# A two-dimensional Fourier mix and a low-rank mixer on one core: the second batch's low-rank step one loop step later, its lines drained by two engines, and the last chunk's output buffers in another pool

## The chip, the cores and the metric

The kernel runs on one core of a Trainium2 chip. The metric is the device time of one execution in microseconds. Five executions of the kernel before are known; beside them there is one execution taken with a profile, which has a time of its own.

## The reference

The input x has 8 batches of 3136 rows and 256 columns. What is computed, cut to what matters:

```python
X = fft(fft(x, axis=1), axis=2).real          # batch, 3136, 256
h = (X^T @ U @ V)^T                           # rank 32, along the 3136 rows
u = X + h
out = u + relu(u @ w_ch1) @ w_ch2             # w_ch1: 256 x 1024, w_ch2: 1024 x 256
```

## The kernel before, in words

The 3136 rows are taken as 49 x 64, so the transform along them is done in two stages: stage one over the 49, on lines of 64, and stage three over the 64, one line for each of 25 values k1 (0 to 24; the mirrored lines come out of the same products as "minus" lines). Batches are worked in four pairs.

**The tiles.** For a batch, `g` holds what stage three reads: partitions 0 to 63 are the stage-one results, partitions 64 to 127 hold the low-rank contribution (64 to 95 for the first 129 columns, 96 to 127 for the rest), the same for each k1. So that stage three can add the low-rank part by the same matmul, 64 rows of `te` (the input's projection on U) are spread over all 25 k1 of `g`. `q` holds the finished lines u of a pair, as the columns of the MLP.

**The main loop.** Each pair has 13 chunks of up to 512 rows, and each chunk takes 4 steps `t`, so a pair has 52 steps, numbered 0 to 51. In a step the program issues, in this order: `mlp1` of the present chunk (L375: 8 matmuls into `hps`, drained by ScalarE with a relu into `hT`, L385), `mlp2` of the chunk before (L387: 8 matmuls of 256 columns and two of 128 into `ops`), then the extra steps that a plan has put there, and last the drain of `ops` (ScalarE copies half into `om`, L406; VectorE writes sum and difference into `ob`, L407 and L408; four stores to HBM from SP, L412). The drain comes at every second step. In the last chunk it comes at every step, with two stores, some of them from ScalarE's queue. The order on every engine is the order of the program: the schedule is manual.

**The plan** (`plan`, L780) is a table of 52 lists. `place(steps, lo, hi)` spreads steps evenly over the slots from lo to hi. In the first pair, which differs from the others, the extras around the change are:

- `turned_steps` (L239), steps 10 to 17: stage one of the second batch by another route (L227 `tps`, 32 narrow matmuls), ScalarE copies into `zt`, and at every second step eight VectorE copies write rows of `g` (L76, `quarter_rows`). The last eight come at step 17.
- `te_single` (L293), step 18: 50 narrow matmuls (L298) of `us` with rows 0 to 63 of `g`, then two VectorE copies into `te` (L269, L270) and three GpSimd copies that spread it over k1 0 to 8, 9 to 16 and 17 to 24 of `g` (L306). This is the low-rank step of the second batch.
- `s3_steps` (L314), 13 steps over 19 to 30: stage three of the second batch (L322). A step takes one group of four k1 and one block of columns, into a PSUM tile of the pool `psd`, and drains it into `q`: as one copy of 128x512 for groups 1 to 5, as two copies of up to 128x256 for group 0, and two of 128x128 in the last step. The two steps of group 0 share a slot. The copies are made by the function handed in.
- `place_next` (L789): loads of the next pair's x (SP loads `xa`, GpSimd gathers `xb`, L99), folds on GpSimd (L144, L145) and on VectorE (L134 to L136) and stage one of the next pair (L185), drained by ScalarE (L73), at steps 17, 18, 19, 20, 22, 23 and on.
- `load_uz`, step 24: two loads from SP (L777).

Matmul outputs of `te_single`, `s3_steps`, stage one and `turned_steps` all take turns in the two buffers of `psd`.

`copy_dve` copies on VectorE. `copy_alt` takes ScalarE and VectorE in turn, beginning with ScalarE; one counter serves all its uses, and the first batch's lines, which use it in steps 1 to 8, leave it even.

**Output buffers.** `ob` comes from `opool`, tag "ob", with four buffers; `xa` comes from `xpool`, tag "xa", with four buffers.

Of the kernel before, what the change touches and what calls it, by code (L numbers as in the profile page):

```python
# [10 lines left out]
FP32 = mybir.dt.float32  # L11
# [11 lines left out]
def kernel(  # L23
# [10 lines left out]
    B, S, D = x.shape  # L34
    R = moe_U.shape[1]
    H = moe_w_ch1.shape[1]
    P = 128
# [10 lines left out]
    xpool = ctx.enter_context(tc.tile_pool(name="xpool", bufs=4))  # L48
# [218 lines left out]
    def te_out(pr, b, ps, c0, s0, spread):  # L267
        te = tes[b]
        nc.vector.tensor_copy(te[64:96, 0:129], ps[c0:c0 + 32, 0, 0:129])  # L269
        nc.vector.tensor_copy(te[96:128, 129:256], ps[s0:s0 + 32, 0, 129:256])  # L270
        spread(pr.g[b], te)
# [21 lines left out]
    def te_single(pr, b, spread, ps=None):  # L293

        ps = ps or psd.tile([P, 2, D], FP32, tag="ps", name="teps")
        for k in range(NK1):
            for s, cs in enumerate([slice(0, 129), slice(129, 256)]):
                nc.tensor.matmul(ps[32 * s:32 * s + 32, 0, cs], us[:, k, s::2], pr.g[b][0:64, k, cs],  # L298
                                 start=(k == 0), stop=(k == NK1 - 1))
        te_out(pr, b, ps, 0, 32, spread)  # L300

    def spread(parts):
        def run(g, te):
            src = te[64:128].bitcast(I32)
            for eng, k0, k1 in parts:
                eng.tensor_copy(g[64:128, k0:k1].bitcast(I32), src.unsqueeze(1).to_broadcast([64, k1 - k0, D // 2]))  # L306
        return run

    def two(row, a, b, n):

        v = row[:, a:a + n]
        return bass.AP(row.tensor, v.offset, [list(v.ap[0]), [b - a, 2], [1, n]])

    def s3_steps(pr, b, evac):  # L314

        if pr.q is None:
            pr.q = qpool[pr.p % 2].tile([P, 2, 6272], BF16, tag="q", name="q")

        def mm(o, k1, blk, st, rows=P, low=None):
            lt = low[:, blk::2] if low is not None else pr.g[b][0:rows, k1, blk::2]  # L320
            r = T[0:rows, k1, 0:64] if k1 == 0 else T[0:rows, k1, :].rearrange("p (s j) -> p s j", s=2)
            nc.tensor.matmul(o, lt, r, start=st, stop=True, skip_group_check=True)  # L322

        def lines(ps, g, blk, rows, low=None):
            for u in range(4):
                us = slice(u * 64, (u + 1) * 64)
                mm(ps[:, 0, us] if 4 * g + u == 0 else ps[:, :, us], 4 * g + u, blk, u == 0 and low is None, rows, low)

        def step(g, blk):
            ps = psd.tile([P, 2, 256], FP32, tag="ps", name="ps")  # L330
            lines(ps, g, blk, P)
            move(ps, g, blk, evac)

        def move_part(ps, g, blk, evac, part):
            lo = 64 if part and g == 0 else 0
            c0 = 3200 + b * 1536 + (4 * g - 1) * 64 if part else b * 1600 + 4 * g * 64
            evac(pr.q[:, blk, c0 + lo:c0 + 256], ps[:, part, lo:256])

        def move(ps, g, blk, evac):
            if g == 0:  # L340
                move_part(ps, g, blk, evac, 0)
                move_part(ps, g, blk, evac, 1)
            else:
                k0 = 4 * g
                evac(two(pr.q[:, blk, :], b * 1600 + k0 * 64, 3200 + b * 1536 + (k0 - 1) * 64, 256), ps[:])

        def last():
            ps = psd.tile([P, 2, 2, 64], FP32, tag="ps", name="ps")
            k1 = NK1 - 1
            for blk in range(2):  # L350
                mm(ps[:, blk], k1, blk, blk == 0)
            for blk in range(2):
                evac(two(pr.q[:, blk, :], b * 1600 + k1 * 64, 3200 + b * 1536 + (k1 - 1) * 64, 64), ps[:, blk])

        yield lines, move_part
        for g in range(6):
            for blk in range(2):
                yield lambda g=g, blk=blk: step(g, blk)
        yield last
# [27 lines left out]
    def mlp2(ch, t, last=False):  # L387
        q, nt = ch.pr.q, len(ch.units) // 2
        if t % 2 == 0 or last:
            ch.po = pso.tile([P, 2, 2, P], FP32, tag="o", name="ops")  # L390
        ps = ch.po[:, 0 if last else t % 2]
        tk = slice(ch.c0 + t * P, ch.c0 + (t + 1) * P)
        for j in range(JT):
            nc.tensor.matmul(ps, ch.h[:, j, t * P:(t + 1) * P], W2[:, j, :],  # L394
                             start=(j == 0 and (t % 2 == 0 or last)), stop=(j == JT - 1), skip_group_check=True)
            if j < 2:
                nc.tensor.matmul(ps[:, j], q[:, j, tk], (Bp if ch.sg > 0 else Bm)[:, j], start=False, stop=False,  # L397
                                 skip_group_check=True)
        if not (last or t % 2 == 1 or t == nt - 1):
            return lambda: None  # L400

        def drain():
            n = 1 if last else t % 2 + 1
            ob = opool.tile([P, 2, D], FP32, tag="ob", name="ob")
            om = opool.tile([P, 2, P], FP32, tag="om", bufs=2, name="om")
            nc.scalar.copy(om[:, 0:n], ch.po[:, 0:n, 1])  # L406
            nc.vector.tensor_tensor(ob[:, 0:n, 0:P], ch.po[:, 0:n, 0], om[:, 0:n], op=AL.add)  # L407
            nc.vector.tensor_tensor(ob[:, 0:n, P:D], ch.po[:, 0:n, 0], om[:, 0:n], op=AL.subtract)  # L408

            def store(i, hf, engine):  # L410
                b, r0 = ch.units[2 * (t - n + 1 + i) + hf]
                engine.dma_start(out=out[b].rearrange("(k2 k1) d -> k1 k2 d", k1=N1)[r0],  # L412
                                 in_=ob[hf * 64:(hf + 1) * 64, i])

            if not last or t == 0:
                for i in range(n):
                    for hf in range(2):
                        store(i, hf, nc.sync)
            else:
                store(0, 0, nc.sync)  # L420
                late.append(lambda: store(0, 1, nc.scalar))
            while last and late and (t == 1 or t == nt - 1):
                late.pop(0)()
        return drain
# [307 lines left out]
    opool = ctx.enter_context(tc.tile_pool(name="opool", bufs=4))  # L732
# [8 lines left out]
    spread_pool = spread([(nc.gpsimd, 0, 9), (nc.gpsimd, 9, 17), (nc.gpsimd, 17, NK1)])  # L741
# [38 lines left out]
    def plan(p):  # L780

        at = [[] for _ in range(NS)]

        def place(steps, lo, hi):
            steps = list(steps)
            for i, s in enumerate(steps):
                at[lo + i * (hi - lo) // len(steps)].append(s)

        def place_next(nx, a, gap, s3lo):  # L789

            s1 = list(s1_steps(nx, copy_act))
            for c, (load, fn, fd) in enumerate(load_steps(nx)):
                for o, f in [(0, load), (4, fn), (7, fd), (9, s1[2 * c]), (10, s1[2 * c + 1])]:
                    at[int(a + gap * c) + o].append(f)
            e = int(a + gap * 7) + 11
            place([lambda: (turn(nx, 0, [(0, 8), (8, NK1)]), turn(nx, 1, whole))], e, e + 1)
            place(te_steps(nx, spread_pool), e, e + 2)
            place(list(s3_steps(nx, 0, copy_dve))[1:], s3lo, NS)

        cur = pairs[p]  # L800
        if p == 0:
            rest = []
            for t, f in zip([1, 2, 2, 3, 4, 5, 5, 6, 8], s3b0[4:]):
                at[t].append(f)
            at[0].append(lambda: w2_fold(0))
            at[2].append(lambda: w2_fold(1))
            place([late_tables], 8, 9)
            place([load_uz], 24, 25)
            place([lambda: rest.append(pair_tables())], 6, 7)
            place([lambda: rest[0]()], 10, 11)  # L810
            place(turned_steps(cur, 1, X1), 10, 18)
            place([lambda: te_single(cur, 1, spread_pool)], 18, 19)
            place(list(s3_steps(cur, 1, copy_dve))[1:], 19, 31)
            place_next(pairs[1], 8, 2.6, 44)
        else:
            place(list(s3_steps(cur, 1, copy_dve))[1:], 3, 18)
            if p + 1 < NP:
                place_next(pairs[p + 1], 0, 3.4, 40)
        return at

    for i in range(len(chunks) + 1):
        cur = chunks[i] if i < len(chunks) else None
# [47 lines left out]
```

## Time and profile before

| | |
|---|---|
| median of five runs | 454.09 us (451.43 to 456.57) |
| the profiled execution's own time | 453.86 us |
| its span, first to last instruction | 452.1 us |
| mean granted TensorE clock | 0.993 |
| TensorE matmul busy | 427.7 us, 95% of the span |
| ScalarE busy | 290.5 us, 64% |
| VectorE busy | 224.3 us, 50% |
| GpSimd busy | 143.1 us, 32% |

How to read it: PE is TensorE's matmuls, PEld its weight loads, DVE is VectorE, ACT is ScalarE, POOL is GpSimd, SP is the engine that issues most of the DMAs. L298 means line 298 of the kernel. In a row of the timeline come the start and the length in microseconds, the engine, the line, the operation, what is written <- what is read, the shapes, how many; in brackets, how long the engine had been idle before it, and what it waited for. The granted clock is the share of TensorE's full speed that it was given.

### The profile page before, as it was taken

To read this page: it belongs to the slowest core of one execution; us is meant where nothing else is said; L and a number is where in the kernel's file an instruction comes from. 1 tells how busy PE (TensorE), PEld (TensorE's weight loads), DVE (VectorE), ACT (ScalarE), POOL (GpSimd) and SP (SyncE) were. 2 spreads that over 40 slices of the span, in tenths; PEclk is the share of its full clock that TensorE was granted. 3 is DMA by queue.
4 is the path that set the end of the run, shared out by engine and by line. 5 is a ranking of instruction groups with operands and counts; after the bars stand their busy time and mean duration, and the time that the engine had idled before them with its cause. 6 is when DMAs were issued, how large, how long until landed. Compare 5 with 4: busy or idle time off the path is not lost.

```text
span 452.1 us, 10536 instructions
## 1 busy us (share of the span) xinstructions
PE 427.7 (95%) x4158; PEld 309.5 (68%) x4221; DVE 224.3 (50%) x541; ACT 290.5 (64%) x402; POOL 143.1 (32%) x180
## 2 busy tenths in 40 slices
PE   3889997999999998999999999999999999999995
PEld 1656665777767776776867777767767777666763
DVE  7773686765345467563354356563354345222222
ACT  5886653777565576777466666777466665666662
POOL 7465355841330546360420444560410000000000
PEclk9999998999999999999999999999999999999998
DMA  8749753875592646763682548763662222222323
GB/s 150 159 134 170 205 157 104 246 195 173 148 241 65 171 117 221 224 186 117 162 213 66 146 128 247 220 190 118 159 141 71 71 63 62 76 71 72 86 56 93
DMA packets 59761, 64.34 MB, mean 142 GB/s; under 512 B 12950, under 2 KB 52672, under 8 KB 59552
## 3 DMA queue, kind: packets, MB, share of 16 engines
q1 hardware_dynamic: 50000, 42.68, 36.7%
q0 software_dynamic: 7232, 14.30, 13.3%
q10 hardware_dynamic: 2480, 6.69, 3.9%
q8 instruction: 33, 0.54, 0.5%
q14 instruction: 16, 0.13, 0.1%
HBM read 34.62 MB, written 32.19 MB: 148 GB/s over the span
## 4 chain that ended last, share of the span: by engine, by line
PE 85%; DVE 6%; DMA 4%; issue 2%; SPq 1%; POOL 1%; ACT 1%; DVEq 0%; POOLq 0%
PE ops L394 35%; PE hps L383 34%; PE ps L322 5%; PE ops L397 4%; PE ps L185 2%; DMA out_dram<-ob 2%; PE teps L284 1%; SPq L412 1%; DMA w_f<-in_moe_w_ch_dram 1%; PE tps L227 1%; DVE g L76 1%; PE teps L298 1%; ACT hT L385 1%; DVE q L76 1%; DVE ob L408 1%
## 5 line engine op out<-in xcount | busy, mean ns | idle before, releaser
L385 ACT ACTIVATE hT<-hps 128x1024 bf16<-128x1024 f32 (+1 forms) x208 | 202.5, 975 | 110.4 <-PE hps L383 103.6
L394 PE MATMUL ops<-W,hT 128*128 128x256 bf16 x1568 | 225.3, 273 | 1.1 <-DVE ob L408 0.9
L394 PEld LDWEIGHTS <-hT 128*128 128x128 bf16 x1568 | 145.4, 98 | 35.4 <-DVE ob L408 0.8
L76 DVE CAST q<-ps 128x512 bf16<-128x512 f32 (+3 forms) x121 | 65.1, 559 | 87.3 <-PE ps L322 81.6
L383 PE MATMUL hps<-q,W1p 128*128 128x512 bf16 (+1 forms) x420 | 103.2, 355 | 2.3 <-DVE q L76 0.5
L407 DVE TENSOR_TENSOR ob<-ops,om 128x256 f32<-128x256 f32 (+1 forms) x102 | 41.8, 410 | 114.7 <-ACT om L406 112.3
L383 PE MATMUL hps<-q,W1m 128*128 128x512 bf16 x351 | 96.4, 381 | 2.2 <-ACT hT L385 0.5
L144 POOL TENSOR_TENSOR y<-xa,xb 98x510 f32<-98x510 f32 (+1 forms) x48 | 61.1, 1294 | 109.1 <-DMA xa<-in_x_dram 87.3
L383 PEld LDWEIGHTS <-W1p 128*128 128x128 bf16 x448 | 40.3, 97 | 26.9 <-issue 1.7
L383 PEld LDWEIGHTS <-W1m 128*128 128x128 bf16 x384 | 35.5, 98 | 27.0 <-issue 2.0
L397 PEld LDWEIGHTS <-q 128*128 128x128 bf16 x392 | 38.5, 98 | 21.7 <-issue 1.2
L406 ACT COPY om<-ops 128x256 f32<-128x256 f32 (+1 forms) x102 | 37.3, 365 | 13.7 <-PE ops L394 7.9
L306 POOL COPY g<-te 64x1024 int32<-64x1024 int32 (+1 forms) x23 | 24.8, 1119 | 57.4 <-DVE te L270 52.8
L408 DVE TENSOR_TENSOR ob<-ops,om 128x256 f32<-128x256 f32 (+1 forms) x102 | 41.1, 403 | 0.0
L73 ACT CAST z<-ps 128x512 bf16<-128x512 f32 x48 | 28.1, 586 | 18.8 <-PE ps L185 17.6
L397 PE MATMUL ops<-Bp,q 128*128 128x128 f16 x200 | 38.4, 219 | 0.0
L322 PE MATMUL ps<-T,g 128*128 128x128 bf16 (+3 forms) x400 | 36.9, 218 | 0.3 <-ACT q L73 0.3
L397 PE MATMUL ops<-Bm,q 128*128 128x128 f16 x192 | 37.1, 220 | 0.0
L322 PEld LDWEIGHTS <-g 128*128 128x128 bf16 (+1 forms) x400 | 29.5, 98 | 4.5 <-DVE q L76 0.4
L99 POOL DMA_INDIRECT xb<-in_x_dram,idx x24 | 24.4, 1018 | 5.4 <-issue 4.3
L185 PE MATMUL ps<-yb,F 98*128 98x258 bf16 (+1 forms) x108 | 19.2, 268 | 1.7 <-DVE q L76 1.7
L76 DVE COPY g<-zt 32x400 bf16<-32x400 bf16 (+3 forms) x45 | 17.0, 378 | 7.2 <-ACT zt L73 6.5
(136 smaller groups left out, 210.8 us busy)
## 6 DMA issues: line engine op xcount, KB each, us to landing
out_dram<-ob SPq DMA_DIRECT2D x389, 64.0 KB
xa<-in_x_dram SPq DMA_DIRECT2D x24, 392.0 KB
zturn<-z ACTq DMA_DIRECT2D x9, 512.0 KB
g<-zturn SPq DMA_DIRECT2D x3, 800.0 KB
g<-zturn SPq DMA_DIRECT2D x3, 544.0 KB
X<-in_x_dram POOLq DMA_DIRECT2D x4, 384.0 KB, 8.2
X<-in_x_dram POOLq DMA_DIRECT2D x2, 744.0 KB
zturn<-z ACTq DMA_DIRECT2D x3, 448.0 KB
```

What stands on the lines that cost most here:

```text
L73: nc.scalar.copy(o, i)
L76: nc.vector.tensor_copy(o, i)
L144: nc.gpsimd.tensor_tensor(ck.y[:, l0:l1, 1:256], ck.xa[:, l0:l1, 1:256], rb[:, l0:l1, 255:0:-1], op=AL.add)
L185: nc.tensor.matmul(o[..., cs], F[:, 2 * t + i].rearrange("p b k c -> p (b k c)"), y[..., cs], start=first, stop=True, skip_group_check=True)
L322: nc.tensor.matmul(o, lt, r, start=st, stop=True, skip_group_check=True)
L383: nc.tensor.matmul(ps[:, i, 0:n], (W1p if ch.sg > 0 else W1m)[jp // 2][:, blk, j], q[:, blk, c0:c0 + n], start=(blk == 0), stop=(blk == 1))
L385: nc.scalar.activation(ch.h[:, 2 * jp:2 * jp + 2, 0:n], ps[:, :, 0:n], AF.Relu)
L394: nc.tensor.matmul(ps, ch.h[:, j, t * P:(t + 1) * P], W2[:, j, :], start=(j == 0 and (t % 2 == 0 or last)), stop=(j == JT - 1), skip_group ...
L397: nc.tensor.matmul(ps[:, j], q[:, j, tk], (Bp if ch.sg > 0 else Bm)[:, j], start=False, stop=False, skip_group_check=True)
L406: nc.scalar.copy(om[:, 0:n], ch.po[:, 0:n, 1])
L407: nc.vector.tensor_tensor(ob[:, 0:n, 0:P], ch.po[:, 0:n, 0], om[:, 0:n], op=AL.add)
L408: nc.vector.tensor_tensor(ob[:, 0:n, P:D], ch.po[:, 0:n, 0], om[:, 0:n], op=AL.subtract)
```

## The change

Two places are changed in the first pair's plan: the low-rank step of the second batch is put at step 19 instead of 18, and its stage three is spread over steps 20 to 30 instead of 19 to 30, drained by ScalarE and VectorE in turn instead of by VectorE alone. And in the last chunk of the kernel the output buffers are taken from the pool and tag of the x loads instead of the output pool.

```diff
         def drain():
             n = 1 if last else t % 2 + 1
-            ob = opool.tile([P, 2, D], FP32, tag="ob", name="ob")
+            ob = (xpool.tile([P, 2, D], FP32, tag="xa", name="ob") if last else
+                  opool.tile([P, 2, D], FP32, tag="ob", name="ob"))
             om = opool.tile([P, 2, P], FP32, tag="om", bufs=2, name="om")
...
             place(turned_steps(cur, 1, X1), 10, 18)
-            place([lambda: te_single(cur, 1, spread_pool)], 18, 19)
-            place(list(s3_steps(cur, 1, copy_dve))[1:], 19, 31)
+            place([lambda: te_single(cur, 1, spread_pool)], 19, 20)
+            place(list(s3_steps(cur, 1, copy_alt))[1:], 20, 31)
             place_next(pairs[1], 8, 2.6, 44)
```

With 13 stage-three steps over 11 slots, slots 20 and 25 get two of them and the others one.

## The prediction

> **What bounds the kernel now.** I read the page first: TensorE is busy 427.7 of 452.1 us and the chain that ended last is 85% PE, so only time in which PE idles or runs slowly can be won. Then the waits by engine, for the places where PE idles behind another engine, then the timeline and the half-microsecond windows of the one place that stands out. From the list of waits (us in total, times, longest):
>
> ```profile
> PE ps L185 <- DVE q L76: 1.7, 2, 1.1
> PE teps L298 <- DVE g L76: 1.5, 1, 1.5
> DVE ob L407 <- DMA out_dram<-ob: 1.3, 3, 0.5
> ```
>
> The second row is the step that the change moves; one of the two waits of the first row lies right behind it; the third is what the output buffers touch. The timeline there (start, length, engine, then what; idle before it in brackets):
>
> ```profile
> 69.16 3.04 DVE L76 COPY g<-zt 32x400 bf16<-32x400 bf16 x8 [0.89 <-ACT zt L73]
> ...
> 69.95 0.82 PE L394 MATMUL ops<-W,hT 128*128 128x256 bf16 x6
> 72.25 1.61 PE L298 MATMUL teps<-g,us 64*32 64x129 bf16 x50 [1.49 <-DVE g L76]
> ...
> 74.63 1.49 PE L383 MATMUL hps<-q,W1m 128*128 128x512 bf16 x3 [0.22 <-issue]
> 75.00 3.12 POOL L306 COPY g<-te 64x1152 int32<-64x1152 int32 x3 [4.60 <-issue]
> ...
> 77.48 0.56 PE L322 MATMUL ps<-T,g 128*128 128x64 bf16 x8
> 77.88 1.28 DVE L76 CAST q<-ps 128x256 bf16<-128x256 f32 x4 [3.00 <-PE ps L322]
> 78.62 0.40 PE L185 MATMUL ps<-yb,F 98*128 98x258 bf16 x2 [0.59 <-DVE q L76]
> ```
>
> Step 18 of the first pair: PE is through with both MLP halves at about 70.7 and stands until 72.25, because the low-rank step needs rows of g that DVE is still copying (eight copies, 69.16 to 72.20). What comes after is slow too. The windows (busy us of PE, PEld, DVE, ACT, POOL; then granted clock):
>
> ```profile
> 73.30:73.80 0.50, 0.50 (x20) 0.37 (x15) 0.50 (x3) 0.00 (x0) 0.00 (x0) 0.89 0.00 0
> 73.80:74.30 0.50, 0.50 (x4) 0.37 (x4) 0.47 (x3) 0.00 (x0) 0.00 (x0) 0.50 0.00 0
> ...
> 76.30:76.80 0.50, 0.50 (x6) 0.38 (x4) 0.00 (x0) 0.50 (x1) 0.50 (x1) 0.50 0.28 74
> 76.80:77.30 0.50, 0.50 (x5) 0.41 (x4) 0.00 (x0) 0.38 (x1) 0.50 (x2) 0.70 0.36 90
> ```
>
> The clock is 0.50 from about 73.75 to 77.1, some 3.4 us, and nowhere else in the main loop (the page's row of clocks has its one low digit there). From the end of the kernel:
>
> ```profile
> 447.89 0.29 DVE L407 TENSOR_TENSOR ob<-ops,om 128x128 f32<-128x128 f32 x1 [0.47 <-DMA out_dram<-ob]
> 448.10 0.28 DVE L408 TENSOR_TENSOR ob<-ops,om 128x128 f32<-128x128 f32 x1
> ...
> 448.34 0.54 SPq L412 DMA_DIRECT2D out_dram<-ob  x1
> 448.97 0.55 SPq L412 DMA_DIRECT2D out_dram<-ob  x1
> ```
>
> The last drain waits for an earlier store, yet SP, which issues the stores, follows on one after another from 443.93 and reaches the last only at 448.97.
>
> **What the Trainium skill says.** (1) "TensorE: Matmul & The Clock Gate", Part 1: the array runs at half rate after a quiet window of about 3.4 us, until a busy one has passed, and the windows run free of the kernel. The trace agrees: 0.50 for 3.4 us after a gap of 1.5 us followed by 1.6 us of narrow matmuls. (2) The same page, "Architectural detail": ScalarE and VectorE are strict FIFO. It agrees: the low-rank step's te copy at 74.28 starts behind the ob pair that ends at 74.25. (3) "GPSIMD Engine Reference", Specifications: GpSimd shares its SBUF interface with VectorE, and instructions with two SBUF inputs collide. The four-element L145 took 0.65 us beside DVE's folds (81.90) and 0.21 alone (91.62).
>
> **The change, part by part.**
>
> *Low-rank step from 18 to 19.* Without it step 18 is two MLP halves, 1.85 us (a step with both extras, 78.86 to 81.15, is 2.29, less 0.22 for L322 and 0.22 for L185), and one L185, 0.22: 68.76 to 70.83. Step 19: 1.85, which ends at 72.68, after DVE's copies (72.20), so PE no longer waits; then the low-rank matmuls, 1.55, and L185, 0.22: to 74.45. Step 20: 1.85, the two s3 groups of g=0 0.44, L185 0.22 behind a wait worked out below as 0.37: to 77.33. Before, step 21 began at 81.15: 3.8 us sooner. One s3 group of 0.22 that had been done by then is still to come: 3.6. The same as removed waits: 1.6 of idle (70.6 to 72.25), 3.4 us at half clock = 1.7, and 0.2 of the L185 wait: 3.5.
>
> *What is late next.* The te copies on DVE (2 x 0.29), then the first POOL spread (1.15). Matmuls end at 74.23; te about 74.45 to 75.03, which is free since the ob pair ends at 74.25; spread 75.15 to 76.30. PE wants g for s3 at 76.30. In the kernel before the slow clock covered this; now there is nothing to spare, and I take 0.05, with 0 to 0.5 if the hand-overs are longer or DVE's ob collides with the spread. The low-rank step holds one psd buffer; its partners (L73 copies at 69.02 and about 71.2) are out in time.
>
> *Queues passed.* te's issue moves behind chunk 4's load: on POOL the indirect gather (0.97) then runs at about 70.5, in idle time (POOL is free from 70.4 to 75.0), instead of at 78.42 behind the spread, so that the next fold starts 1 us sooner. On SP the matching xa load still waits behind four stores of the drain that DVE ends at 74.25, so stays at 76.8; its fold ran at 83.94 without waiting for it. No DMA is added.
>
> *Two engines drain.* 16 evacuations, DVE's alone until now: 0.32 each for g=0 (4 in 1.28), 0.69 for 128x512. Half go to ACT. For g=0 the two parts of a buffer are drained side by side, so L185 waits about 0.59 - 0.22 = 0.37. The price is ACT: two copies of 0.37 (row L406), five of 0.585 (row L73), one small 0.3: 4.0 us over steps 20 to 30. ACT is busy 12.9 of 18 us there (84 to 102), 72%; 4.0 over 24.5 us adds 16 points: 88%, and real spacings are shorter (a relu of 1.03 is followed after 0.92). A q copy puts the next relu off by at most 0.5 us; its reader, the second MLP half a step later, has about 1.1 us left. So I cost it at nothing; were that slack used up, it would cost up to 4.0. The last s3 step stays at 30 and chunk 6 reads groups 0 and 1 (steps 20 to 22) at step 24.
>
> *Output buffers.* The fourth drain no longer waits: 0.29 sooner (om ends at 447.57, ob began at 447.89). SP's last store is bound by the stores before it (448.34 + 0.54), and starts at 448.97, so nothing of it reaches the end. Bounds 0 and 0.3; I take 0. The xa buffers have been free since the last fold, so no new wait is seen.
>
> Sum: 1.6 + 1.7 + 0.2 - 0.05 = 3.5. Against the execution's own 453.86 (span 452.1 and 1.8 around it) that is 450.4; the median of the five runs is 454.09, which gives **450.6**, 0.8% faster. About 1% (4.5 us) is what a measurement of this kernel can tell from no change, so most of this case counts as no change.
>
> **Rivals.**
> - *A, as above: 450.6.* For it: PE has next to no other waits behind it, and later work is paced by PE. 60%.
> - *B, the clock still drops.* The narrow low-rank matmuls may count as quiet, or a free-running window catches them. Against it: the first low-rank step (23.7 to 25.3), with little idle before it, kept clock 1.00. Gain 1.6 + 0.2: 452.2. 15%.
> - *C, the lead is given back.* The last x load (SP, 103.29, behind UZ loads of 5.0 us and stores) feeds a fold that ends at 111.0 and the ob behind it at 112.07; step 36 wants its buffer at 113.70, 1.6 us of slack. If DMA keeps that load where it is, PE waits 3.5 - 1.6 = 1.9: 452.5. Against it: until 92 SP waits for drains, so UZ and the load move along. 10%.
> - *D, slower.* ACT becomes the bound in steps 20 to 30: its 12% of idle isn't usable in order, relus come late, and the 4.0 us of copies land on the path against 3.5 won: 454.6, or 456 with B's clock. It decides once relu lags by more than 1.1 us at a chunk's end. 7%.
> - *E, more:* the end's 0.3, no L185 wait (0.37) and load waits eased: 449.8. 8%.
>
> **How the numbers follow.** A's own range is 449.3 to 451.9, from the 0 to 0.5 of the spread, the 0.3 at the end, and a median over runs that spread from 451.4 to 456.6. B and C reach to 453.4, and below A I allow for E: 448.9 to 453.4 for 8 in 10. Faster by over 1% (below 449.5) takes a fifth of A and half of E, 0.17; slower by over 1% (above 458.6) only D with noise, 0.05; the rest 0.78.
>
> **What would show it.** Right: L298 starts at about 72.7 with no wait for DVE g; clock 1.00 from 72 to 78; L322's first group at about 76.3 with a wait for POOL of at most 0.3; ACT near 88% between 77 and 100 and no PE wait for hT there; step 24 (first W1p matmuls, 87.82 before) at about 84.2 and the end 3.5 us sooner; the last SP store still bound by the one before. Wrong: a clock of 0.5 near 75 (B); PE idle between 105 and 115 (C); PE waiting for ACT between 77 and 100 (D); a last store that moved ahead of the rest.

## The result, and the profile after

The changed kernel takes 450.78 us in the median of 42 runs (449.46 to 454.67); the kernel before, in 79 runs beside it, 453.72. The ratio is 0.9947, with a 95% interval of 0.9935 to 0.9960: 2.4 us or half a per cent faster, within the 1% that was called no change. That is the difference of the means (453.5 and 451.1 us); the medians are 2.9 us apart. The median was forecast to 0.2 us, the gain (3.5 us) too high. The profiled execution has a span of 449.6 us against 452.1, and a mean clock of 1.000 against 0.993.

From the list of PE's waits in the changed kernel (three of its rows; from L404 on its line numbers are one higher than before):

```profile
PE ps L185 <- DVE q L76: 1.7, 2, 1.1
PE teps L298 <- DVE g L76: 0.5, 1, 0.5
PE ps L185 <- ACT q L73: 0.5, 1, 0.5
```

The wait of 1.5 us before L298 is gone (the 0.5 us left in that row belongs to the first batch's low-rank step, ahead of the loop). The row of L185 is as long as before, and a new one, for ScalarE's `q`, stands beside it. The timeline of steps 18 to 20 (the first MLP half of a step is four matmuls, L383, not the eight of the description above):

```profile
68.93 3.30 DVE L76 COPY g<-zt 32x400 bf16<-32x400 bf16 x8 [0.65 <-ACT zt L73]
...
71.80 0.82 PE L394 MATMUL ops<-W,hT 128*128 128x256 bf16 x6
...
72.55 1.59 PE L298 MATMUL teps<-g,us 64*32 64x129 bf16 x50
...
74.52 0.81 PE L383 MATMUL hps<-q,W1m 128*128 128x512 bf16 x3
...
75.03 3.11 POOL L306 COPY g<-te 64x1152 int32<-64x1152 int32 x3 [3.41 <-DVE te L270]
...
76.23 0.57 PE L322 MATMUL ps<-T,g 128*128 128x64 bf16 x8
...
76.64 0.65 ACT L73 CAST q<-ps 128x256 bf16<-128x256 f32 x2 [0.25 <-PE ps L322]
...
77.04 0.63 DVE L76 CAST q<-ps 128x192 bf16<-128x192 f32 x2 [0.89 <-ACT q L73]
77.45 0.38 PE L185 MATMUL ps<-yb,F 98*128 98x258 bf16 x2 [0.66 <-DVE q L76]
```

PE comes to L298 at 72.55, after VectorE's eight copies (72.23), and goes straight through. The end of the list is a surprise: ScalarE and VectorE don't drain the first group side by side. VectorE's first copy starts when ScalarE's has ended, and L185 waits 0.66 us, where 0.37 was forecast. The clock in the windows of two microseconds (busy us of PE, PEld, DVE, ACT, POOL; granted clock):

```profile
72.00:74.00 2.00, 2.00 (x56) 1.71 (x54) 1.97 (x6) 0.69 (x1) 0.00 (x0) 1.00 0.71 180
74.00:76.00 2.00, 1.94 (x20) 1.36 (x16) 1.47 (x5) 1.50 (x3) 0.96 (x1) 1.00 0.21 61
76.00:78.00 2.00, 1.34 (x15) 0.87 (x14) 1.11 (x4) 1.16 (x4) 2.00 (x3) 1.00 0.39 98
```

It stays at 1.00. Some of what was won is given back in steps 24 and 25:

```profile
82.69 3.18 DVE L134 TENSOR_TENSOR yb<-y 98x508 bf16<-98x508 f32 x1
82.81 2.50 POOL L144 TENSOR_TENSOR y<-xa,xb 98x510 f32<-98x510 f32 x2
...
86.38 0.17 DVE L136 CAST yb<-y 98x8 bf16<-98x8 f32 x1
86.61 0.11 PEld L185 LDWEIGHTS <-F 98*128 98x128 f16 x2 [0.21 <-issue]
...
88.69 0.61 PE L322 MATMUL ps<-T,g 128*128 128x128 bf16 x8
...
89.12 0.59 ACT L73 CAST q<-ps 128x512 bf16<-128x512 f32 x1 [0.18 <-PE ps L322]
...
89.75 0.38 PE L185 MATMUL ps<-yb,F 98*128 98x258 bf16 x2 [0.45 <-ACT q L73]
```

In step 24 L185 reads a fold that VectorE ends at 86.55. The first instruction of that fold, 0.68 us when alone, took 3.18 (82.69 to 85.87) and ended just after GpSimd's own fold (82.81 to 85.31). In step 25, which has two groups of stage three and an L185, the third output finds both `psd` buffers taken until ScalarE has drained the first.

**A measure without the noise of the front.** The start of step 18 differs between executions by 3.7 us (67.2 to 70.9 us in the thirteen traces used here), for reasons that lie ahead of the loop: the six latest (69.4 us and later) are those in which PE stands 2.0 to 2.8 us there, up to about 20 us, and five of these then run 3.4 us at half clock. So I measure in each trace from the first L383 of step 18 to the first L383 of step 31, before and after which the kernels do the same; a missing record puts such a start off by 0.1. Before: 68.76 to 103.33, 34.6 us. After: 68.53 to 100.89, 32.4. The difference of 2.2 is kept to the end: from step 18 to the last matmul it is 378.45 against 376.24.

At the kernel's end the fourth drain now waits for `om` alone (first row), and SP's last store (the other view) still comes right behind the store before it:

```profile
445.15 0.29 DVE L408 TENSOR_TENSOR ob<-ops,om 128x128 f32<-128x128 f32 x1 [0.17 <-ACT om L407]
```

```profile
445.89 0.56 SPq L413 DMA_DIRECT2D out_dram<-ob  x1
446.54 0.55 SPq L413 DMA_DIRECT2D out_dram<-ob  x1
```

From the last matmul's end to the last store's start it is 1.77 us (444.77 to 446.54), before 1.76 (447.21 to 448.97).

### The profile page after: what moved, and what is told of

It is laid out like the page before. It is cut to its first block, busy times and chain, and to the rows that moved or that the text cites. A ratio compares the mean times of both kernels' runs of the same rounds, so it can differ in the third digit from the quotient of the medians.

```text
span 449.6 us, 10529 instructions
## 1 busy us (share of the span) xinstructions
PE 426.6 (95%) x4159; PEld 309.1 (69%) x4221; DVE 226.6 (50%) x533; ACT 293.6 (65%) x410; POOL 143.8 (32%) x180
## 4 chain that ended last, share of the span: by engine, by line
PE 88%; DVE 5%; issue 3%; ACT 2%; DMA 1%; POOL 0%; SPq 0%; DVEq 0%; POOLq 0%; ACTq 0%
PE ops L394 37%; PE hps L383 35%; PE ps L322 5%; PE ops L397 5%; PE ps L185 3%; PE tps L227 1%; PE teps L284 1%; DVE g L76 1%; ACT hT L385 1%; PE teps L298 1%; DMA out_dram<-ob 1%; DVE q L76 1%; ACT zt L73 0%; DVE ta L448 0%; DVE ob L408 0%
## 5 line engine op out<-in xcount | busy, mean ns | idle before, releaser
L383 PE MATMUL hps<-q,W1p 128*128 128x512 bf16 (+1 forms) x421 | 103.2, 355 | 2.3 <-DVE q L76 0.5
L76 DVE CAST q<-ps 128x512 bf16<-128x512 f32 (+3 forms) x113 | 60.8, 558 | 83.5 <-PE ps L322 78.9
L383 PE MATMUL hps<-q,W1m 128*128 128x512 bf16 x351 | 95.5, 379 | 2.1 <-ACT hT L385 0.5
L144 POOL TENSOR_TENSOR y<-xa,xb 98x510 f32<-98x510 f32 (+1 forms) x48 | 62.2, 1315 | 106.8 <-DMA xa<-in_x_dram 86.0
L383 PEld LDWEIGHTS <-W1p 128*128 128x128 bf16 x448 | 40.3, 97 | 26.9 <-issue 1.7
L383 PEld LDWEIGHTS <-W1m 128*128 128x128 bf16 x384 | 35.3, 98 | 26.5 <-issue 1.4
L322 PE MATMUL ps<-T,g 128*128 128x128 bf16 (+3 forms) x400 | 36.8, 218 | 0.3 <-ACT q L73 0.3
L322 PEld LDWEIGHTS <-g 128*128 128x128 bf16 (+1 forms) x400 | 29.3, 98 | 4.6 <-DVE q L76 0.4
L134 DVE TENSOR_TENSOR yb<-y 98x508 bf16<-98x508 f32 (+1 forms) x24 | 23.9, 998 | 0.2
L135 DVE TENSOR_TENSOR yb<-y 98x508 bf16<-98x508 f32 (+1 forms) x24 | 22.8, 951 | 0.0
```

The lines of the kernel that those rows point to most:

```text
L76: nc.vector.tensor_copy(o, i)
L144: nc.gpsimd.tensor_tensor(ck.y[:, l0:l1, 1:256], ck.xa[:, l0:l1, 1:256], rb[:, l0:l1, 255:0:-1], op=AL.add)
L383: nc.tensor.matmul(ps[:, i, 0:n], (W1p if ch.sg > 0 else W1m)[jp // 2][:, blk, j], q[:, blk, c0:c0 + n], start=(blk == 0), stop=(blk == 1))
```

## The experiments

The ratios are to the kernel before, run beside each of the three sets (one chip for each set), with intervals of 95%; steps 18 to 31 come from one profiled execution of each kernel.

**The parts alone.** The first: the move and the spacing, all drains on VectorE.

```diff
-            place([lambda: te_single(cur, 1, spread_pool)], 18, 19)
-            place(list(s3_steps(cur, 1, copy_dve))[1:], 19, 31)
+            place([lambda: te_single(cur, 1, spread_pool)], 19, 20)
+            place(list(s3_steps(cur, 1, copy_dve))[1:], 20, 31)
```

> The low-rank step at 19 and stage three over 20 to 30, drained by VectorE alone; output buffers as before. Theory (the move carries the gain, the two engines give nothing): ratio to the kernel before 0.993 to 0.996, the same as the whole change (0.9947); clock 1.00 from 72 to 78 us; the two waits of L185 in the steps with two stage-three groups (20 and 25) about 0.6 us each, as with two engines. Rival (the two-engine drain is needed for the gain): L185 waits of 1 us or more, ratio 0.997 to 1.000.

Measured: 0.9983 (0.9965 to 1.0002), clock 1.00 from 66 to 84 us, steps 18 to 31 33.2 us. My theory falls: in this set the move alone doesn't bring the gain. (The changed kernel's second measurement, 0.9968 below, overlaps with this one, so that the ratios alone would leave it open; steps 18 to 31 are 33.2 us against its 32.3 and 32.4.) The rival was right in the ratio and not in place: L185 waits 0.59 and 0.56 us, no more than in the changed kernel; what is new are short stops elsewhere (its timeline):

```profile
84.15 2.58 DVE L134 TENSOR_TENSOR yb<-y 98x508 bf16<-98x508 f32 x1
...
87.33 0.68 DVE L76 CAST q<-ps 128x512 bf16<-128x512 f32 x1
88.06 0.38 PE L322 MATMUL ps<-T,g 128*128 128x128 bf16 x4 [0.51 <-issue]
```

VectorE stands in a drawn-out fold and its `q` copies queue behind. The profile names nothing that L322 waited for, but it starts 0.05 us after the copy that frees its buffer (88.01), 0.51 us late.

The second: only the drain by two engines.

```diff
-            place(list(s3_steps(cur, 1, copy_dve))[1:], 19, 31)
+            place(list(s3_steps(cur, 1, copy_alt))[1:], 19, 31)
```

> Only the drain by two engines in turn, the low-rank step at 18 as before. Theory: nothing of the gain, ratio 0.999 to 1.001, the stop of about 1.5 us before L298 and the half clock after it stay, the wait of L185 behind the two groups of k1 0 to 3 stays at about 0.6 us. Rival (side-by-side drains win something by themselves): that wait falls to 0.35 us or less and the ratio is 0.998. Rival (ScalarE gets crowded): PE waits for relus, ratio above 1.002.

Measured: 0.9985 (0.9957 to 1.0014), steps 18 to 31 33.5 us. By this ratio nothing can be said of an effect. The stop before L298 stays (1.49 us), the wait of L185 is 0.66, not 0.35. But the half clock did not stay: this trace shows 1.00 from 74 to 84 us.

The third: only the output buffers.

```diff
-            ob = opool.tile([P, 2, D], FP32, tag="ob", name="ob")
+            ob = (xpool.tile([P, 2, D], FP32, tag="xa", name="ob") if last else
+                  opool.tile([P, 2, D], FP32, tag="ob", name="ob"))
```

> Only the output buffers of the last chunk from the x load pool. Theory: the last drain starts 0.3 us sooner after the one before, SP's last store stays bound by the stores before it, ratio 0.9995 to 1.0005. Rival (the drain's wait reaches the end): 0.3 us, ratio 0.9993 and a last store that starts 0.3 us sooner against the last matmul.

Measured: 0.9984 (0.9963 to 1.0005). The interval holds both expectations, so the trace decides: the last store starts 1.77 us after the last matmul, as before. Its middle is the kernel before unchanged, so that this trace is also a second look at the kernel before. Its timeline and, below it, its windows:

```profile
71.43 1.59 PE L298 MATMUL teps<-g,us 64*32 64x129 bf16 x50 [1.47 <-DVE g L76]
```

```profile
72.00:74.00 2.00, 2.00 (x42) 1.43 (x37) 1.96 (x7) 0.59 (x1) 0.00 (x0) 1.00 0.03 8
74.00:76.00 2.00, 1.76 (x19) 1.19 (x17) 0.27 (x2) 1.02 (x1) 1.83 (x2) 1.00 0.30 78
76.00:78.00 2.00, 1.48 (x11) 0.95 (x12) 1.21 (x5) 1.04 (x3) 1.70 (x3) 1.00 0.57 116
```

The same stop, and the clock keeps 1.00. Steps 18 to 31 take 33.5 us here, 1.1 less than in the first trace of the kernel before. The three parts, and the filled kernel below, all came out between 0.9983 and 0.9986 in this set, this one too, which moves nothing in the loop: such ratios don't rank the parts.

**The clock by itself.** Six matmuls of 128x512 in the idle time of step 18, into the tile that L298 then overwrites:

```diff
+        fill = b == 1
         ps = ps or psd.tile([P, 2, D], FP32, tag="ps", name="teps")
+        for i in range(6 if fill else 0):
+            nc.tensor.matmul(ps[:], W1p[0][:, 0, 0:P], W1p[0][:, 1, :].rearrange("p (a d) -> p a d", d=D),
+                             start=True, stop=True, skip_group_check=True)
```

> The kernel before, with six matmuls of 128x512 into the low-rank step's PSUM tile ahead of its own, which overwrite it: 1.3 us of work in the 1.5 us in which PE stands idle in step 18. Nothing else is moved. Theory (the half clock comes from that idle time and costs its own 1.7 us): L298 still starts about when VectorE's copies end, the clock stays 1.00 from 72 to 78 us, ratio 0.996 to 0.997. Rival (the narrow matmuls of the low-rank step pull the clock down by themselves): clock 0.5 for 3.4 us as before, ratio 1.000. Rival (the clock fell only in some executions): between the two, 0.998.

Measured: 0.9986 (0.9959 to 1.0013), which holds all three expectations. Its one trace is of its longest execution (457.99 us), and no time is taken from it; it shows the edit in place, with the six matmuls from 73.33 to 74.79.

The question can be followed further by other means, since every execution has a mean clock. With (1 - clock) x span as the lost clock, the kernel before lost 1.98 us on average over the 209 executions of these three sets (0.10 standard error), the changed kernel 1.22 over 66 (0.12). In the third set, where both ran on one chip, it was 2.20 (75 executions, 0.17) and 1.45 (22, 0.24). The filled kernel lost 1.66 (15, 0.34), the kernel before beside it 1.73 (59, 0.20), so no effect of the filling is seen here either. That the half clock follows the stop in some executions and not in all is what the traces say: one of the three that have it.

The mean clock does not say where it was lost. In some traces it is 0.50 only after the last matmul, where this costs nothing; in five it is 0.50 for 3.4 us ahead of the loop, between 20 and 26 us, behind a long stop of PE as in the trace of the spaced kernel below:

```profile
20.46 2.14 PE L227 MATMUL tps<-Fs,X 98*32 98x100 f16 x119 [2.51 <-issue]
```

Of the thirteen traces, six have a stop of 2.0 to 2.8 us there, and the five are among these; the seven with at most 1.4 us keep 1.00.

So the change saves 0.8 us of lost clock on average, and rather less of time: with the clock held, other waits come out that it had covered (1.1 us between the two traces of 34.6 and 33.5, for a fall of 3.4 us at half rate). Most of the gain is there without it: executions with a mean clock of 0.998 or more take 452.67 us on average in the kernel before (61, standard error 0.15) and 450.86 in the changed one (34, 0.16), 1.8 us less.

**What gives back the rest.** Four edits on the changed kernel. The spacing: the double steps where no L185 stands.

```diff
-            place(list(s3_steps(cur, 1, copy_alt))[1:], 20, 31)
+            for t, f in zip([20, 21, 21, 22, 23, 24, 25, 26, 26, 27, 28, 29, 30],
+                            list(s3_steps(cur, 1, copy_alt))[1:]):
+                at[t].append(f)
```

> The changed kernel with its 13 stage-three steps on 20, 21, 21, 22 to 25, 26, 26, 27 to 30: the steps with two groups are 21 and 26, which have no L185, instead of 20 and 25, which have one. Theory (two groups and an L185 in one step outrun the two psd buffers): the waits of L185 for q (0.66 and 0.62 us in the changed kernel) are gone or under 0.2, steps 18 to 31 take 31.3 us instead of 32.4 and the ratio to the kernel before is 0.992 to 0.993. Rival (PE waits for VectorE, whose folds are drawn out by GpSimd, and only the place of the wait moves): steps 18 to 31 stay at 32 us or more, with waits elsewhere, ratio 0.9945.

Measured: 0.9936 (0.9914 to 0.9957), steps 18 to 31 31.8 us. Both waits of L185 are gone. Much of that came back as one wait of L322 for VectorE's `q`, behind a fold of 4.2 us (79.00 to 83.22 in its timeline):

```profile
83.51 0.38 PE L322 MATMUL ps<-T,g 128*128 128x128 bf16 x4 [0.88 <-DVE q L76]
```

Theory and rival each have a half.

Each buffer by one engine:

```diff
-            move(ps, g, blk, evac)
+            move(ps, g, blk, evac[blk] if isinstance(evac, tuple) else evac)
...
-            place(list(s3_steps(cur, 1, copy_alt))[1:], 20, 31)
+            place(list(s3_steps(cur, 1, (copy_act, copy_dve)))[1:], 20, 31)
```

> The changed kernel with each buffer of stage three drained by one engine (the first block of columns by ScalarE, the second by VectorE) instead of copies in turn, which differs for the first group alone: there the two parts of one buffer had gone to two engines, and the trace shows VectorE's copy waiting for ScalarE's. Theory (the two copies of one buffer run one after the other, on two queues): L185 in step 20 waits 0.6 us still or somewhat more, since two copies of a buffer follow one another either way; ratio 0.9945 as the changed kernel. Rival (that hand-over between engines is what makes the wait): 0.35 us, steps 18 to 31 shorter by 0.3.

Measured: 0.9973 (0.9953 to 0.9993), steps 18 to 31 32.3 us, L185 in step 20 waits 0.48 us. It lies between the two, and nothing is won.

The folds of two chunks a step sooner:

```diff
-                for o, f in [(0, load), (4, fn), (7, fd), (9, s1[2 * c]), (10, s1[2 * c + 1])]:
+                for o, f in [(0, load), (4, fn), (6 if nx.p == 1 and c in (2, 3) else 7, fd), (9, s1[2 * c]), (10, s1[2 * c + 1])]:
```

> The changed kernel with VectorE's folds (L134 to L136) of the third and fourth chunk one step sooner, when GpSimd is not at its own folds (L144). Theory (the two engines' folds hold each other up, and the late fold costs PE 0.2 us in step 24): L134 to L136 of these two chunks take 1.5 to 2 us each instead of 4, the wait in step 24 is gone, steps 18 to 31 shorter by 0.2 to 0.3. Rival (VectorE has room and its folds' length costs nothing): the folds shorten and steps 18 to 31 stay at 32.4. Rival (the length of a fold has nothing to do with GpSimd): the folds stay long.

Measured: 1.0027 (1.0008 to 1.0045), steps 18 to 31 35.1 us: slower than before. No expectation held, since the folds only met other work of GpSimd's:

```profile
76.43 4.02 POOL L306 COPY g<-te 64x1152 int32<-64x1152 int32 x3 [3.68 <-DVE te L270]
76.94 1.63 DVE L135 TENSOR_TENSOR yb<-y 98x508 bf16<-98x508 f32 x1
...
78.49 1.02 DVE L136 CAST yb<-y 98x8 bf16<-98x8 f32 x1
80.22 0.61 DVE L76 CAST q<-ps 128x192 bf16<-128x192 f32 x2
...
80.62 0.38 PE L185 MATMUL ps<-yb,F 98*128 98x258 bf16 x2 [1.97 <-DVE q L76]
...
84.26 2.92 DVE L136 CAST yb<-y 98x8 bf16<-98x8 f32 x1
84.62 2.50 POOL L144 TENSOR_TENSOR y<-xa,xb 98x510 f32<-98x510 f32 x2
```

It shows the link all the same. VectorE's fold beside GpSimd's spread drags on, the `q` copies queued behind it come at 80.22, and PE waits 1.97 us, and 1.04 more for a later one. A cast of 8 elements takes 2.92 us beside GpSimd's fold, and 0.17 alone.

The three edits together:

> The three edits together on the changed kernel. Theory: steps 18 to 31 take 31.0 to 31.3 us, ratio to the kernel before 0.991 to 0.993. Rival (something else holds the rest): 32 us and 0.9945.

Measured: 1.0050 (1.0031 to 1.0070), steps 18 to 31 36.1 us, with one long wait of L185 for VectorE's `q`:

```profile
85.69 0.59 PE L185 MATMUL ps<-yb,F 98*128 98x258 bf16 x2 [3.16 <-DVE q L76]
```

The sooner folds outweigh the other two edits. After this stop the clock is 0.50 from 85.7 to 89.1 us, which is part of the 36.1.

**Taking the drains off VectorE.** The spacing again, with the first two groups drained by ScalarE alone and the later ones by block (shown against the spaced kernel, and cut: the function that picks the engine is asked for each group and block):

```diff
-                            list(s3_steps(cur, 1, copy_alt))[1:]):
+                            list(s3_steps(cur, 1, lambda g, blk: copy_dve if g > 1 and blk else copy_act, True))[1:]):
```

> As the spaced kernel (stage three on 20, 21, 21, 22 to 25, 26, 26, 27 to 30), with the first two groups, four buffers, drained by ScalarE alone, and the later groups by block (first block ScalarE, second VectorE). VectorE then has no evacuation to make before step 24, the time in which its folds are held up by GpSimd's. Theory (the rest of the loss is VectorE standing in its folds with an evacuation queued behind): steps 18 to 31 take 31.0 us (30.6 would be no wait at all) and the ratio to the kernel before is 0.990 to 0.993. Rival (ScalarE gets crowded there): PE waits for ScalarE's q or relus, 31.8 us or more.

Measured: 0.9938 (0.9917 to 0.9958), median 450.50 us, steps 18 to 31 30.8 us, with no wait of PE at all between 68 and 106 us (windows, columns as above):

```profile
78.00:80.00 2.00, 2.00 (x20) 1.44 (x18) 1.84 (x4) 2.00 (x6) 2.00 (x2) 1.00 0.95 335
80.00:104.00 24.00, 24.00 (x207) 17.48 (x205) 14.93 (x28) 18.72 (x30) 13.86 (x16) 1.00 0.75 211
```

VectorE's folds are as long as ever (4.2 us, 75.32 to 79.50); no copy that PE waits for is queued behind them. The theory's steps came out, its ratio not quite: it is the spaced kernel's (0.9936), measured on another chip, so that the microsecond between 31.8 and 30.8 us is seen in the traces alone.

The same spacing on VectorE alone:

> The same spacing, low-rank step at 19, all of stage three drained by VectorE. Theory (VectorE is held in its folds and what is queued behind comes late): PE waits of 1 us or more for q between 76 and 92 us, steps 18 to 31 take 32.5 us or more, ratio 0.996 to 0.999. Rival (spacing alone is what matters): 31.8 us as the spaced kernel with two engines, ratio 0.994.

Measured: 0.9955 (0.9936 to 0.9975), steps 18 to 31 32.6 us. The row that decides is PE's:

```profile
81.92 0.40 PE L322 MATMUL ps<-T,g 128*128 128x128 bf16 x4 [1.21 <-DVE yb L136]
```

The wait is there as the theory has it: the profile puts it down to the last instruction of the fold (80.05 to 81.29), and the `q` copies queued behind that one run from 81.19. The ratio lies between the two numbers. Here a comparison within one set is possible: the mean time is 451.83 us (standard error 0.25), and 450.45 (0.29) with the drains taken off VectorE as above.

All drains of the changed kernel on ScalarE (`copy_act` in place of `copy_alt`):

> The changed kernel with all of stage three drained by ScalarE. Theory (VectorE's holds are worse than a full ScalarE): no wait for VectorE's q; steps 18 to 31 take 32.0 to 32.8 us; the ratio is like the changed kernel's, 0.994 to 0.996, though ScalarE is over 90% busy. Rival (ScalarE becomes the bound, the slower case of the prediction): PE waits for relus (hps or ops for hT) and steps 18 to 31 take 33.5 us or more, ratio 0.998 or above.

Measured: 0.9948 (0.9928 to 0.9968), steps 18 to 31 31.9 us.

```profile
80.00:104.00 24.00, 23.55 (x206) 17.30 (x205) 13.94 (x24) 21.71 (x36) 14.70 (x16) 1.00 0.75 211
```

ScalarE is busy 21.7 of 24 us, and PE never waits for a relu; its two waits are L185's in the double steps, 0.48 and 0.45.

The changed kernel again, beside these three:

> The changed kernel once more, beside the three others on one chip. Theory: ratio 0.993 to 0.997; steps 18 to 31 take 32.4 us within 0.3; the clock keeps 1.00 from 70 to 78 us. Rival (its first trace was a lucky one): the half clock after the low-rank step is there again.

Measured: 0.9968 (0.9948 to 0.9988), median 452.35 us, steps 18 to 31 32.3 us, clock 1.00 throughout. The version with the spacing and ScalarE first has a mean span 1.4 us shorter than this (448.66 and 450.10 over 22 executions each, standard errors 0.29 and 0.27). It beats both kernels.

## Why the prediction was right or wrong

- **The median.** Its 0.2 us is partly luck. The five executions that the forecast started from have a median 0.4 us above that of the 79, and the gain was forecast 0.6 us above the 2.9 between the medians; the two nearly cancel.
- **The idle time, 1.6 us.** Right: L298 starts at 72.55 with no wait for VectorE, as worked out (72.7). The steps after it went as worked out too, up to step 24 (84.34 for 84.2).
- **The half clock, 1.7 us.** Right for the execution that the sum was made against, whose time it is. Not shown, and likely too much, when carried to the median: "3.4 us at half clock = 1.7" takes an event of one execution for a property of the kernel. Two other traces with the same stop keep 1.00, and over all executions the change saves 0.8 us of lost clock. The prediction had quoted from the Trainium skill that the windows run free of the kernel ("TensorE: Matmul & The Clock Gate", Part 1), and used that only against the changed kernel (rival B), not for the kernel before. It also took the trace to agree. That holds for the length of the half clock, 3.4 us; a stop of 1.5 us is less than the quiet window of 3.4 us that the page gives, and what else counted as quiet no run here shows. (The profile's row of clocks has a second low digit, its last, which lies after the last matmul.)
- **The two-engine drain of the first group, 0.37.** Wrong by 0.29: the two parts of a buffer are drained one after the other. The Trainium skill has it, in "PSUM — Partial Sum Buffer", section "PSUM bank collisions raise a hardware error": two engines may not touch one bank and quadrant at once, two readers included, and the compiler adds a dependency. The trace agrees (VectorE's copy of the first buffer starts at 77.04, 0.40 us after ScalarE's and when that has ended), and in step 25, with two buffers, the two engines do drain side by side (89.12 to 89.71 and 89.34 to 90.03). That this dependency, and not another between the two copies, made the wait isn't shown.
- **The double step 25.** It was seen in the plan and costed at nothing. It has two groups and an L185 like step 20, and costs 0.6 (it takes 3.13 us, 86.84 to 89.97, for 1.85 + 0.44 + 0.22 of work). This is the largest of the terms that were left out, and the spaced kernel shows it: with the groups moved, the wait is gone.
- **GpSimd's spread, 0.05:** 0.20 measured, within the 0 to 0.5 given.
- **VectorE's folds.** Not in the sum. The prediction named the shared SBUF interface and used it for the spread alone. With GpSimd's folds 0.7 to 1.2 us sooner than before and VectorE's 3.1 to 4.2, the two meet: 3.18 us for a fold of 0.68, and 0.2 in step 24.

The last four come to 0.29 + 0.6 + 0.15 + 0.2 = 1.2 of the 1.3 us between the 3.5 forecast and the 2.2 seen between the two traces.

- **"So I cost it at nothing"**, of the two engines: right that PE never waits for a relu in these steps, but the two engines also win, for which the sum had only the 0.2 of the L185 wait. With VectorE alone the move gives 33.2 us for steps 18 to 31 in place of 32.4. ScalarE's part takes work out of a queue that is held up. ScalarE was busy 17.82 of the 23 us from 77 to 100, 77% where 88% was forecast.
- **The output buffers, 0.** Right: the drain is 0.3 us sooner and SP's last store is where it was.
- **The rivals.** B: not in either trace of the changed kernel; its executions still lose 1.22 us of clock on average. Where isn't known for these; in four of the edited kernels with the low-rank step at 19 the trace has the half clock ahead of the loop. C: no; the last x load's fold on GpSimd moved from 107.16 to 103.60 with the rest, and steps 31 to 40 take 17.6 us in both. D: no; even with all drains on ScalarE PE never waits for a relu. E: no.

What stays open: the gain of 2.4 us is more than what the traces account for with the clock held (33.5 to 32.4). Executions of high clock differ by 1.8 us, so that some 0.7 us of the gain isn't found in steps 18 to 31. One trace or two for each kernel, and a noise of some 0.2% in each ratio, don't settle it. That the stop of 1.5 us causes the half clock behind it is argued from one trace in three; filling it changed nothing that could be measured. Whether the folds' meeting could be had out of the way by moving GpSimd's side wasn't tried.

## What to carry to other kernels

When a stop is removed, cost every place in which the moved work meets the same limit again: here a step with two groups and a third output on two buffers, twice. An event that the clock or a collision makes in one execution has a chance as well as a price; weigh it before it goes into a forecast of the median. And where an engine's instructions are drawn out by a neighbour, look at what is queued behind them: taking the drains out of that queue won 1 us in the traces (31.8 to 30.8), where doing the held instructions sooner lost time.

## What the runs showed of the hardware

- A VectorE instruction from SBUF that met GpSimd's two-input fold ended only with that fold or just after it: 0.68 us became 3.18, and an 8-element cast of 0.17 us became 2.92. GpSimd's spread was drawn out too (4.02 us for 3.11).
- An idle time of 1.5 us followed by 1.6 us of narrow matmuls was followed by 3.4 us at half clock in one trace of the three that have it. Ahead of the loop a stop of 2.0 to 2.8 us was followed by it in five traces of six, one of at most 1.4 us in none of seven.
- Two copies of one PSUM buffer on ScalarE and VectorE ran one after the other (from 76.64 and 77.04); copies of two buffers ran side by side (89.12 to 89.71 and 89.34 to 90.03).
